# Keys and values of two row chunks by seven block products

## The chip, the cores and the metric

The kernel runs on one core of a Trainium2 chip. The metric is device time in microseconds (us), the median of several runs. A core has a matrix engine (TensorE, PE in the profile, with its weight loads as PEld), a vector engine (VectorE, DVE), a scalar engine (ScalarE, ACT), GpSimd (POOL) and a queue that only issues transfers here (SyncE, SP). Each works through its own list of instructions in order and waits on semaphores of the others. Tiles lie in SBUF; matmuls write to PSUM, in banks of 128x512 float32.

## The reference, cut to what matters

```python
# S = 2048 rows, D = 512, H = 32 heads of 16, F = 1792
q, k, v = x @ wqkv                        # per head
phi(t) = concat(softmax(t @ w_phi), softmax(-t @ w_phi))
kv = phi(k).T @ v ;  z = sum_s phi(k)     # per head, over all rows
a = (phi(q) @ kv / (phi(q) @ z + 1e-6)) @ wo
b = relu(x @ w1 + b1)**2 @ w2 + b2
g = sigmoid((x * gate_w).sum(-1))
out = g * a + (1 - g) * b
```

## The kernel before

Every large float32 product is made of three passes in the format float32r: an operand is split into a high part (a copy by ACT) and a low part (the operand minus the high part, by DVE), and `mm3` adds high times high, high times low and low times high in one PSUM bank. `split` is the line pair 61 and 64 of the profile.

The rows of x stand in four blocks (`NB`) of four chunks (`NC`) of 128 rows. The hidden width stands in 14 parts of 128; the work list runs over two sweeps of seven parts, four blocks each: 56 entries. For each entry `up` makes one 128x512 bank of the hidden layer (12 matmuls), two entries ahead (`LAG`), ACT and DVE make the squared relu and its split (`hidden`), and `down` adds 12 matmuls to four banks `d0` to `d3` that stay open for seven entries. This is the frame; everything of the attention is hung between by `at(slot, f)`, two slots for an entry.

In the first sweep that is keys and values. `do_fold` multiplies the key weights with the feature map (`fold`, plain float32 matmuls), `do_w` loads the value weights, and for each of the 16 chunks `do_k` makes 12 matmuls and `exps` (two reductions and two subtractions by DVE out of PSUM, an exponential by ACT, a sum and a reciprocal by DVE, then `scaled` on POOL, line 214), `do_v` makes 12 matmuls and one ACT copy into `vext` (line 411), and `do_kv` adds two chunks' 64 small matmuls to `kvps`. Keys and values take turns in one bank (`ps_a`; `ps_b` holds `kvps`), so the bank must be read out before the next of them starts. The second sweep does queries, numerators and the output projection in the same way.

What sets the order: the framework orders each engine's list from the program's order, with `high_priority(offset=AHEAD)` pulling the read-outs forward; what stands in the lists is fixed, and at run time an engine only waits. All loads and stores go through SP in order, into a ring of four staging tiles (`in`) and six `row` tiles.

Of the kernel before, what the change touches and what calls it, by code (L numbers as in the profile page):

```python
# [28 lines left out]
AHEAD = 150  # L29


@with_exitstack
def tile_gated_mix(ctx: ExitStack, tc: tile.TileContext, xT, xn, wqT, wkT, wphi, wv, wo, w1, b1, w2, b2, gw, out):
# [88 lines left out]
    part = dram.tile([NB * NC, P, D], F32, name="part")  # L122
    zrow = dram.tile([2 * D], F32, name="zrow")
# [15 lines left out]
    def fold(loaded, nm, k):  # L139
# [9 lines left out]
        return hi, lo  # L149

# [41 lines left out]
    def exps(ps, tag="e"):  # L192

        pv = ps.rearrange("p (h f) -> p h f", f=DH)
        mx = small.tile([P, H], F32, tag="mx", name="mx")
        mn = small.tile([P, H], F32, tag="mn", name="mn")
        e = work.tile([P, H, 2, DH], F32, tag=tag, name="e", bufs=2 if tag == "e" else 1)
        bc = lambda t: t.unsqueeze(2).to_broadcast([P, H, DH])
        with tc.high_priority(offset=AHEAD):
            nc.vector.tensor_reduce(mx, pv, AX.X, ALU.max)  # L200
            nc.vector.tensor_reduce(mn, pv, AX.X, ALU.min)
            nc.vector.tensor_tensor(e[:, :, 0, :], pv, bc(mx), ALU.subtract)
            nc.vector.tensor_tensor(e[:, :, 1, :], bc(mn), pv, ALU.subtract)  # L203
# [15 lines left out]
    def kv_chunk(n, kvps, phi, v):  # L219
        for i in range(NG):  # L220
            for j in range(4):
# [3 lines left out]
                                 start=(n == 0 and i == 0), stop=(n == NB * NC - 1),  # L225
# [86 lines left out]
    def up(fc, xs, wf):  # L312
        ps = ps_u.tile([P, SB], F32, tag="u", name="u")
        for k in range(NK):
            up_step(ps, k, xs, wf)
        return hidden(fc, ps)
# [8 lines left out]
    def do_fold(nm, k):  # L325
        with tc.issue_after(st["up"].ins):
            st["wa", nm, k] = fold(st["wT"], nm, k)
        if k == NK - 1:
            st["wa"] = [st["wa", nm, i] for i in range(NK)]
            if nm == "k":  # L330
                banks.pop()

# [69 lines left out]
    def do_k(b, c):  # L402

        n = b * NC + c
        e3, r = exps(project(c, st["x", b], st["wa"], "k"), "ez" if n % NV == NV - 1 else "e")
        st["phi", n] = scaled(e3, r, nc.gpsimd)

    def do_v(b, n, c):
        ps = project(c, st["x", b], st["wb"], "v")
        with tc.high_priority(offset=AHEAD):  # L410
            nc.scalar.activation(heads(vext[n % NV])[:, :, :DH], ps.rearrange("p (h f) -> p h f", f=DH), AF.Copy)

    def do_kv(n):
        if n == 0:
            st["kv"] = ps_b.tile([P, 2 * P], F32, tag="s", name="kvps")
        for m in (n, n + 1):
            kv_chunk(m, st["kv"], st["phi", m], vext[m % NV])
# [51 lines left out]
    def at(slot, f, *a):  # L469
        steps.setdefault(int(slot), []).append(lambda: f(*a))  # L470
# [7 lines left out]
    for k in range(NK):  # L478
        at(3 + k // 2, do_fold, "k", k)
    at(1, do_w, wv, "v")  # L480
    for b in range(NB):
# [5 lines left out]
        for c in range(NC):  # L487
# [128 lines left out]
```

## Time and profile before

| | |
|---|---|
| three runs | 530.46, 531.08, 531.87 us; median 531.08 |
| span of the profiled execution, first to last instruction | 528.2 us; no separate device time of that execution is listed, the median lies 2.9 us above its span |
| granted TensorE clock | 1.000 |
| busy: PE, PEld, DVE, ACT, POOL | 519.0, 417.6, 356.5, 234.1, 77.0 us |
| moved by the main queue | 44.20 MB, 26.8% of 16 engines' time |

The busy time of PE is a share of the span in which at least one matmul is under way; a matmul's row is longer than the distance to the next one, since they are pipelined. The distance between starts tells the rate. "Idle before" and the list of waits say who ended an engine's idle time. In a timeline a row gives start and duration in us; rows of one engine can overlap a little.

### The profile page before, as it was taken

The numbers are of one execution on the slowest core, as the hardware profiler recorded it, in microseconds if no ns is written. First come the engines' busy times: TensorE is split into PE (matmuls) and PEld (weight loads), VectorE is DVE, ScalarE is ACT, GpSimd is POOL, SyncE is SP. The second block draws the span as 40 slices with busy tenths as digits, with TensorE's granted clock in tenths as the row PEclk, the third lists the DMA queues.
The fourth block names the chain that finished last, engine by engine and source line by source line (L and its number), as shares of the span: only waits on it lengthen the run. The fifth ranks groups of instructions, "written<-read, shape, count | busy, mean of one in ns | idle before, by whom it ended". The sixth has DMA issues, their size and how long they took to land.

```text
span 528.2 us, 8945 instructions
## 1 busy us (share of the span) xinstructions
PE 519.0 (98%) x3475; PEld 417.6 (79%) x3475; DVE 356.5 (68%) x608; ACT 234.1 (44%) x404; POOL 77.0 (15%) x61
## 2 busy tenths in 40 slices
PE   8998999999999999999999999999999999999997
PEld 4876888888888888888878878787887878787785
DVE  4688546833656334566769897998878887779423
ACT  4874424623335234354644663463435353535230
POOL 2001111111111111011103121102011111112000
PEclk9999999999999999999999999999999999999999
DMA  7974004200032000434346114134102311022102
GB/s 255 297 234 131 1 1 161 81 2 1 24 138 79 2 0 22 159 85 137 81 146 215 34 40 124 66 107 130 45 17 89 113 49 30 24 77 94 47 1 79
DMA packets 30834, 45.16 MB, mean 86 GB/s; under 512 B 5704, under 2 KB 12360, under 8 KB 30792
## 3 DMA queue, kind: packets, MB, share of 16 engines
q1 hardware_dynamic: 30328, 44.20, 26.8%
q8 instruction: 27, 0.44, 0.4%
q10 hardware_dynamic: 432, 0.39, 0.2%
q14 instruction: 15, 0.12, 0.1%
q0 software_dynamic: 32, 0.01, 0.0%
HBM read 29.89 MB, written 8.39 MB: 72 GB/s over the span
## 4 chain that ended last, share of the span: by engine, by line
PE 63%; DVE 15%; DMA 7%; ACT 5%; SPq 5%; issue 2%; POOL 2%; DVEq 0%; POOLq 0%; ACTq 0%
PE u L69 6%; PE u L71 6%; PE u L70 6%; PE d L71 6%; PE d L70 6%; PE d L69 6%; SPq L259 4%; PE k L69 3%; PE v L69 2%; PE k L70 2%; PE k L71 2%; PE v L70 2%; PE v L71 2%; DMA in<-in_w 2%; PE att L69 2%
## 5 line engine op out<-in xcount | busy, mean ns | idle before, releaser
L305 ACT ACTIVATE r<-u,b1c 128x512 f32<-128x512 f32 x56 | 38.5, 687 | 152.1 <-PE u L71 143.5
L69 PE MATMUL d<-w2h,hh 128*128 128x512 f32 x224 | 87.5, 390 | 0.0
L69 PE MATMUL u<-xh,w1h 128*128 128x512 f32 x220 | 86.8, 395 | 0.4 <-ACT w1h L61 0.4
L70 PE MATMUL d<-w2l,hh 128*128 128x512 f32 x224 | 87.2, 389 | 0.0
L71 PE MATMUL d<-w2h,hl 128*128 128x512 f32 x224 | 87.2, 389 | 0.0
L71 PE MATMUL u<-xh,w1l 128*128 128x512 f32 x220 | 85.8, 390 | 0.1
L70 PE MATMUL u<-xl,w1h 128*128 128x512 f32 x220 | 85.7, 390 | 0.0
L64 DVE TENSOR_TENSOR hl<-r,hh 128x512 fp32r<-128x512 f32 x56 | 42.8, 764 | 55.9 <-ACT hh L61 55.9
L233 POOL TENSOR_TENSOR ez<-e,z 128x512 f32<-128x512 f32 x32 | 41.4, 1316 | 187.7 <-ACT e L205 187.7
L214 POOL TENSOR_TENSOR e<-e,r 128x1024 f32<-128x1024 f32 x16 | 32.4, 2025 | 202.1 <-DVE r L210 144.8
L208 DVE TENSOR_REDUCE sm<-e 128x64 f32<-128x1024 f32 x32 | 39.0, 1217 | 28.5 <-ACT e L205 28.3
L69 PEld LDWEIGHTS u<-xh,w1h 128*128 128x128 f32 x220 | 41.3, 188 | 12.2 <-ACT hh L61 1.6
L71 PEld LDWEIGHTS d<-w2h,hl 128*128 128x128 f32 x224 | 42.1, 188 | 8.7
L69 PEld LDWEIGHTS d<-w2h,hh 128*128 128x128 f32 x224 | 42.0, 188 | 8.7
L70 PEld LDWEIGHTS d<-w2l,hh 128*128 128x128 f32 x224 | 42.1, 188 | 8.6
L71 PEld LDWEIGHTS u<-xh,w1l 128*128 128x128 f32 x220 | 41.3, 188 | 9.1 <-DVE w1l L64 0.6
L70 PEld LDWEIGHTS u<-xl,w1h 128*128 128x128 f32 x220 | 41.3, 188 | 8.2
L205 ACT ACTIVATE e<-e 128x1024 f32<-128x1024 f32 x32 | 33.8, 1055 | 23.2 <-DVE e L203 22.4
L257 ACT ACTIVATE phiT<-tb 32x256 f32<-32x256 f32 x64 | 26.4, 413 | 34.6 <-DVE tb L251 33.9
L61 ACT ACTIVATE hh<-r 128x512 fp32r<-128x512 f32 x56 | 35.2, 628 | 1.3
L306 ACT ACTIVATE r<-r 128x512 f32<-128x512 f32 x56 | 35.1, 627 | 1.0
L566 DVE SCALAR_TENSOR_TENSOR row<-d,rest,row 128x512 f32<-128x512 f32 (+1 forms) x33 | 22.4, 731 | 8.5 <-PE d L71 8.5
(106 smaller groups left out, 875.4 us busy)
## 6 DMA issues: line engine op xcount, KB each, us to landing
in<-in_xT SPq DMA_DIRECT2D x32, 256.0 KB, 3.8
in<-in_w SPq DMA_DIRECT2D x24, 256.0 KB, 3.1
phiT<-tb SPq DMA_DIRECT2D x192, 32.0 KB, 1.8
row<-in_xn SPq DMA_DIRECT2D x16, 256.0 KB, 2.8
part<-row SPq DMA_DIRECT2D x16, 256.0 KB, 2.0
row<-part SPq DMA_DIRECT2D x16, 256.0 KB, 3.7
out<-row SPq DMA_DIRECT2D x15, 256.0 KB, 2.3
row<-in_wkT SPq DMA_DIRECT2D x4, 256.0 KB, 5.8
```

Of the source, the lines that this page charges most:

```text
L61: i = nc.scalar.activation(hi, src, AF.Copy)
L64: elo.tensor_tensor(lo, src, hi.bitcast(F32), ALU.subtract)
L69: nc.tensor.matmul(o, ah[:, sa], bh[:, sb], start=first, stop=False)
L70: nc.tensor.matmul(o, ah[:, sa], bl[:, sb], start=False, stop=False)
L71: return nc.tensor.matmul(o, al[:, sa], bh[:, sb], start=False, stop=last)
L205: nc.scalar.activation(ef, ef, AF.Exp)
L208: nc.vector.tensor_reduce(sm, e3, AX.X, ALU.add)
L214: eng.tensor_tensor(e3, e3, w.unsqueeze(2).to_broadcast([P, 2 * H, DH]), ALU.mult)
L233: nc.gpsimd.tensor_tensor(ez[:, hs, :], e3[:, hs, :], zbc[half], ALU.mult)
L257: nc.scalar.activation(dst, src, AF.Copy)
L305: nc.scalar.activation(r, ps, AF.Relu, bias=b1c[:, fc:fc + 1])
L306: nc.scalar.activation(r, r, AF.Square)
```

## The change

Two chunks c and c+2 of a block make a pair (eight in all). Their rows, cut in two halves of the inner width (256), are a 2x2 block matrix; the weights are laid side by side, half the columns of the folded key weights and half of the value weights in one 512-wide operand, and are a 2x2 block matrix too. Keys and values of a pair are then made by the Strassen-Winograd scheme: seven block products of six matmuls each, 42 instead of 48.

- `joint_weights` (slots 3 and 4) copies the folded keys out of PSUM beside the value columns (`raw`), splits seven operands for each half j, and makes four differences for each half on POOL (`sub`). Operands 1, 2, 5, 7 stay in SBUF (`HELD`); 6, 3 and 4 (`KEPT`) take turns in one place (`oh`, `ol`), are written to DRAM (`wkeep`), and are read back by `again` before each of their products: four transfers of 256 KB each, except for product 6 of pair 0.
- `sums` reads the pair's rows of x again from DRAM, makes four sums on POOL and splits them.
- `pair_steps` sets the products in the order 1, 2, 6, 5, 3, 7, 4, all in the bank of `ps_a`; 2 is added onto 1 and 4 onto 7 in the bank. `u2` and `u4` (`sums` tile) keep partial sums in SBUF. `place` writes the four results to the tiles `e` and `vext`, in halves of 16 heads (128x256).
- `exps` reads the keys from SBUF there, in place, and not from PSUM.
- Slots have halves now: a step may stand in the middle of `up` or after the second chunk of `down`.

```diff
-        at(3 + k // 2, do_fold, "k", k)
-    at(1, do_w, wv, "v")
+    at(3, do_joint, 0)
+    at(4, do_joint, 1)
...
+    def joint_weights(loaded):
...
+            r = raw[k] = work.tile([P, 2 * D], F32, tag="ez" if k == 1 else "e", name=f"raw{k}", bufs=1 if k == 1 else 2)
+            nc.sync.dma_start(two(r)[:, :, 256:], two(wv[k * P:(k + 1) * P, :]))
...
+            nc.scalar.activation(two(r)[:, :, :256], two(ps), AF.Copy)
...
+            split(src, hi, lo, nc.scalar, nc.vector)
+            st["W"][i, j] = hi, lo
+            if i in KEPT:
+                for hl, x in enumerate((hi, lo)):
+                    nc.sync.dma_start(wkeep[KEPT.index(i), j, hl], x.bitcast(F32))
...
+        def first(j):
+            whole(j)
+            whole(2 + j)
...
+            operand(1, j, a)
+            operand(2, j, c)
+            operand(3, j, d)
+            sub(a, b, a)
+            sub(b, d, b)
+            sub(d, d, a)
+            operand(5, j, a)
+            operand(7, j, b)
+            sub(c, c, d)
+            operand(4, j, c)
+            operand(6, j, d)
...
+    def sums(p):
...
+        nc.sync.dma_start(a, rows[:, :2])
+        nc.sync.dma_start(d, rows[:, 2:])
...
+        add(d1, a1, d1, ALU.add)
+        add(a1, a0, a1, ALU.subtract)
+        add(a0, d1, a0, ALU.subtract)
+        add(d0, d0, a0, ALU.subtract)
...
+        split(a, sh[:, 0], sl[:, 0], nc.scalar, nc.vector)
+        split(d, sh[:, 1], sl[:, 1], nc.scalar, nc.vector)
...
+    def again(i):
+        for j in range(2):
...
+                nc.sync.dma_start(x.bitcast(F32), wkeep[KEPT.index(i), j, hl])
...
+    def place(t, half, src, other=None):
...
+                if other is None:
+                    nc.scalar.activation(o, of(src), AF.Copy)
+                else:
+                    nc.vector.tensor_tensor(o, of(other), of(src), ALU.add)
...
+        at(s - 1, sums, p)
+        for off, f in zip((0, 1, 1.5, 2.5, 3.5, 4.5, 5), (p1, p2, p6, p5, p3, p7, p4)):
+            at(s + off, f)
+        at(s + 3.5, phi, n)
+        at(s + 5, phi, m)
+        at(s + 7.5, kv)
...
+    for p in range(NB * NC // 2):
+        pair_steps(p, 5.5 + 5.65 * p)
```

The lists of three engines show what the prediction speaks of. A name with a number is one buffer; "waits" names the engines or transfer semaphores a row waits for.

POOL, from the start of the kernel, before (`w1l0_130` is the low part of the first hidden weight, `e` the features of a chunk):

```order
L127 MEMSET vext2_110 128x32
L64 TENSOR_TENSOR w1l0_130<-row_128,w1h0_129 128x384 [waits DMAHW2_49,DVE_49]
L214 TENSOR_TENSOR e_470<-e_470,r_478 128x1024 [waits DVE_49,Activation_49]
L214 TENSOR_TENSOR e_557<-e_557,r_565 128x1024 [waits DVE_49,Activation_49]
L214 TENSOR_TENSOR e_655<-e_655,r_663 128x1024 [waits DVE_49,Activation_49]
```

The first feature scaling follows directly on the first hidden weight.

POOL at the same place, changed (`raw0` to `raw3` are the joint weights before their sums, `in_486` and `in_487` the rows of x of pair 0):

```order
L182 TENSOR_TENSOR raw0_328<-raw0_328 128x512 [waits DMAHW2_49,DVE_49]
L182 TENSOR_TENSOR raw0_328<-raw2_336,raw0_328 128x512 [waits DMAHW3_49,Pool_49]
L182 TENSOR_TENSOR raw2_336<-raw2_336,raw0_328 128x512 [waits DVE_49,Pool_49]
L182 TENSOR_TENSOR raw2_336<-raw2_336 128x512 [waits Pool_49]
L182 TENSOR_TENSOR raw1_400<-raw1_400 128x512 [waits DMAHW7_49,DVE_49]
L182 TENSOR_TENSOR raw1_400<-raw3_408,raw1_400 128x512 [waits DMAHW3_49,Activation_49,Pool_49]
L476 TENSOR_TENSOR in_487<-in_486,in_487 128x2x128 [waits DMAHW4_49,DMAHW6_49,DMAHW1_49,DVE_49]
L477 TENSOR_TENSOR in_486<-in_486 128x2x128 [waits DMAHW5_49,DMAHW0_49,Pool_49]
L478 TENSOR_TENSOR in_486<-in_487,in_486 128x2x128 [waits Pool_49]
L479 TENSOR_TENSOR in_487<-in_487,in_486 128x2x128 [waits Pool_49]
L182 TENSOR_TENSOR raw3_408<-raw3_408,raw1_400 128x512 [waits DVE_49]
L182 TENSOR_TENSOR raw3_408<-raw3_408 128x512 [waits Pool_49]
```

Twelve operations of POOL stand ahead of the first feature scaling that were not there.

PE, before, at the second chunk's keys (`k_542` is their bank, `wkh0` a part of the folded weights):

```order
L71 MATMUL d0_303<-w2h3_245,hl_342 128x512
L69 MATMUL d1_304<-w2h3_245,hh_341 128x512
L69 MATMUL k_542<-wkh0_356,xh0_0_136 128x512 [waits Activation_49]
L70 MATMUL k_542<-wkl0_357,xh0_0_136 128x512
L71 MATMUL k_542<-wkh0_356,xl0_0_137 128x512
L69 MATMUL k_542<-wkh1_365,xh0_1_153 128x512
```

Here PE waits for one thing, the read-out of the bank by ACT.

PE, changed, about the same number of matmuls from the start, at the second half of product 6 and the start of product 5 of pair 0 (`w61_448` and `w61_449` are high and low part of operand 6 for j = 1):

```order
L505 MATMUL p6_583<-w61_448,sh_494 128x512 [waits Activation_49]
L71 MATMUL u_613<-xh0_1_154,w1h6_542 128x512
L72 MATMUL u_613<-xl0_1_155,w1h6_542 128x512
L73 MATMUL u_613<-xh0_1_154,w1l6_543 128x512
L506 MATMUL p6_583<-w61_449,sh_494 128x512 [waits DVE_49]
L507 MATMUL p6_583<-w61_448,sl_495 128x512
L71 MATMUL u_613<-xh0_2_165,w1h6_542 128x512
L72 MATMUL u_613<-xl0_2_166,w1h6_542 128x512
L73 MATMUL u_613<-xh0_2_165,w1l6_543 128x512
L71 MATMUL u_613<-xh0_3_174,w1h6_542 128x512
L505 MATMUL p5_605<-w50_361,sh_494 128x512 [waits DVE_49]
```

PE now waits for the last weight that is made, high part by ACT and low part by DVE, and ahead of product 5 for DVE's read-out of the bank.

ACT in the middle of the first sweep, before (`v_1189` is a bank of values, `r` and `hh` the hidden layer, `e_1137` the features of a chunk):

```order
L205 ACTIVATE e_1137<-e_1137 128x1024 [waits DVE_49,Pool_49]
L305 ACTIVATE r_1182<-u_1169,b1c_98 128x512 [waits PE_49]
L306 ACTIVATE r_1182<-r_1182 128x512 [waits Activation_49]
L61 ACTIVATE hh_1185<-r_1182 128x512 [waits Activation_49]
L411 ACTIVATE vext2_110<-v_1189 128x32x16 [waits PE_49]
```

ACT in the middle of the first sweep, changed, at pair 3 (`p1_1397` is the bank of products 1 and 2, `e_1340` the features of pair 2's second chunk):

```order
L533 ACTIVATE sums_454<-p1_1397 128x512 [waits PE_49]
L260 ACTIVATE e_1340<-e_1340 128x1024 [waits DVE_49]
L360 ACTIVATE r_1418<-u_1405,b1c_98 128x512 [waits PE_49]
L361 ACTIVATE r_1418<-r_1418 128x512 [waits Activation_49]
L524 ACTIVATE e_1438<-p1_1397 128x16x16 [waits PE_49]
L524 ACTIVATE vext0_109<-p1_1397 128x16x16
```

Two read-outs of the bank enclose an exponential that waits for DVE.

176 lines of the change are left out of this document (138 added, 38 removed).

## The prediction

> **What bounds the kernel now.** First the page's busy times and the windows of the whole span, then PE's waits, then the rows of PE one by one.
>
> ```profile
> PE 519.0 (98%) x3475; PEld 417.6 (79%) x3475; DVE 356.5 (68%) x608; ACT 234.1 (44%) x404; POOL 77.0 (15%) x61
> ```
> ```profile
> 20.00:30.00 10.00, 9.75 (x58) 8.23 (x57) 8.24 (x18) 8.74 (x18) 0.00 (x0) 1.00 0.81 261
> 30.00:40.00 10.00, 10.00 (x45) 8.26 (x44) 8.66 (x23) 7.26 (x16) 0.00 (x0) 1.00 0.75 238
> 40.00:60.00 20.00, 18.58 (x81) 14.80 (x80) 16.01 (x41) 9.76 (x19) 3.87 (x2) 1.00 0.26 84
> 100.00:120.00 20.00, 20.00 (x90) 16.57 (x89) 9.09 (x17) 6.10 (x9) 1.94 (x1) 1.00 0.16 54
> ```
> ```profile
> PE k L69 <- ACT vext L411: 1.1, 1, 1.1
> PE v L69 <- DVE e L203: 0.3, 1, 0.3
> ```
> ```profile
> 29.46 0.48 PE L69 MATMUL u<-xh,w1h 128*128 128x512 f32 x1
> 48.77 0.39 PE L70 MATMUL d<-w2l,hh 128*128 128x512 f32 x1
> 58.74 0.39 PE L69 MATMUL k<-wkh,xh 128*128 128x512 f32 x1
> 61.23 0.39 PE L71 MATMUL k<-wkh,xl 128*128 128x512 f32 x1
> ```
>
> The columns of the windows are PE, PEld, DVE, ACT, POOL, clock, DMA share and GB/s. PE is full from 60 us on (100:120 stands for that stretch), and its waits in the first sweep are small. The keys' rows at 58.74 and 61.23 are eleven matmuls apart: 0.227 us each. So a matmul taken out is worth 0.227 us, and a wait put in costs its length: PE's order is fixed, and it has no slack to give a wait back. The other fact is 20 to 40 us: there ACT and DVE are over 70% busy and POOL does nothing. The change puts its new work exactly there.
>
> **The matmuls.** Eight pairs, six fewer each: 48 by 0.227 = 10.9 us less. The folds and the 64 small matmuls of a pair stay. If all else is covered the kernel ends at 520.2.
>
> **The start.** The first pair's products need weights made by ACT copies, splits and eight differences on POOL, and the pair's row sums (four more). The rows that price this:
>
> ```profile
> 25.14 0.58 ACT L61 ACTIVATE wkh<-foldk 128x512 fp32r<-128x512 f32 x1
> 28.41 0.68 DVE L64 TENSOR_TENSOR hl<-r,hh 128x512 fp32r<-128x512 f32 x1
> 29.01 0.69 DVE L64 TENSOR_TENSOR w2l<-in,w2h 128x512 fp32r<-128x512 f32 x1
> 44.61 2.23 DVE L64 TENSOR_TENSOR hl<-r,hh 128x512 fp32r<-128x512 f32 x1
> 253.00 0.63 DVE L64 TENSOR_TENSOR hl<-r,hh 128x512 fp32r<-128x512 f32 x1
> 253.55 2.42 DVE L64 TENSOR_TENSOR w2l<-in,w2h 128x512 fp32r<-128x512 f32 x1
> ```
> ```profile
> 44.36 1.93 POOL L214 TENSOR_TENSOR e<-e,r 128x1024 f32<-128x1024 f32 x1 [36.46 <-DVE ge L179]
> 253.25 2.17 POOL L214 TENSOR_TENSOR e<-e,r 128x1024 f32<-128x1024 f32 x1 [12.49 <-DVE r L210]
> ```
> ```profile
> L233 POOL TENSOR_TENSOR ez<-e,z 128x512 f32<-128x512 f32 x32 | 41.4, 1316 | 187.7 <-ACT e L205 187.7
> L64 POOL TENSOR_TENSOR w1l<-row,w1h 128x384 fp32r<-128x384 f32 x1 | 1.0, 1012 | 4.1 <-DVE w1h L63 4.1
> L208 DVE TENSOR_REDUCE sm<-e 128x64 f32<-128x1024 f32 x32 | 39.0, 1217 | 28.5 <-ACT e L205 28.3
> ```
>
> A low part on DVE takes 0.60 us when the next follows (28.41 to 29.01). But beside POOL it does not run: at 44.61 it began under a POOL operation that ended at 46.29 and finished at 46.84, 0.55 after it; at 253.25 POOL waited for the running DVE row, went ahead of the next one, and that one ended 0.55 after POOL. So the two take turns, one whole instruction each. This is told of operations with both inputs in SBUF, as all low parts here; reductions keep their 1217 ns.
>
> In the changed DVE list, from the first low part of a joint weight (`w10_345`) to the last (`w61_449`), 29 operations have two SBUF inputs: 25 low parts and four gate products. POOL's twelve must lie between them, for they need the first and the last needs them. ACT's first fold read-out stands at 25.14; in the new list three others follow before `w10` is copied, 0.52 apart, so DVE begins at about 27.4. POOL: eight of 1.30 (the 128x512 row) and four of 256 elements, about 0.7 (between 1.01 for 384 and half of 1.3): 13.2 us. DVE: 29 by 0.60 = 17.4 at most, with half a microsecond of tiny rows; where a turn changes, only some 0.40 are added (0.55 less the 0.15 by which POOL started early), so at least 12 by 0.40 and 17 by 0.60 = 15.0. The last weight is ready between 55.6 and 58.5 us. From there to the first matmul of product 5 are six matmuls or one read-out, 1.4 us: 57.1 to 60.0.
>
> That matmul is the 77th after the folds by the order, so 76 lie before it. The 77th of before is the row at 48.77, the first is that at 29.46. The second fold's start and length I leave as they are. The loss against before is therefore 8.3 to 11.2 us; I take 9.8, since nothing in the order prefers one end. Other steps are inside this: ACT has 36 rows from `w10` to `w61`, some 17 us by 0.52, less than the port's turns; the SP writes of operands 3 and 4 must land before the next one is split into the same place, 2.0 us each by the row below, while DVE works on other splits. If POOL were out of the way, these chains would be the bound (rival one).
>
> The Trainium skill, SBUF — State Buffer, section Who interferes with whom, says that a DVE instruction with two SBUF inputs and a GpSimd instruction that reads SBUF exclude each other, and the second to start fully blocks. It speaks against this change: by it the sum of the start is the 9.8 above, while POOL's idle column alone (nothing from 20 to 40 us) would give about 1.
>
> **The steady pairs.** One bank serves all seven products, so each product waits for the read-out of the one before.
>
> ```profile
> 61.66 0.69 DVE L200 TENSOR_REDUCE mx<-k 128x32 f32<-128x512 f32 x1 [3.13 <-PE k L71]
> ```
> ```profile
> 45.29 0.57 ACT L411 ACTIVATE vext<-v 128x512 f32<-128x512 f32 x1
> 45.92 0.50 PE L69 MATMUL k<-wkh,xh 128*128 128x512 f32 x1 [1.09 <-ACT vext L411]
> ```
> ```profile
> L205 ACT ACTIVATE e<-e 128x1024 f32<-128x1024 f32 x32 | 33.8, 1055 | 23.2 <-DVE e L203 22.4
> L411 ACT ACTIVATE vext<-v 128x512 f32<-128x512 f32 x16 | 9.5, 594 | 25.9 <-PE v L71 25.9
> L178 ACT ACTIVATE ge<-lg 128x1 f32<-128x1 f32 x16 | 3.0, 194 | 9.7 <-DVE row L176 9.7
> L566 DVE SCALAR_TENSOR_TENSOR row<-d,rest,row 128x256 f32<-128x256 f32 x2 | 0.9, 480 | 0.6 <-PE d L71 0.6
> ```
>
> A read-out starts 0.43 us after the last matmul's start (61.23 to 61.66), and PE goes on 0.06 after its end. Half a bank takes 0.39 us on ACT (between 194 and 594 ns) and 0.48 on DVE, so two halves need about 0.7 and 0.9. The order leaves at least six matmuls between, 1.59 us with the last one's own: enough for 1.10 us of read-out. An idle engine makes it.
>
> The place that fails is `place` of product 2 on ACT, with six matmuls behind it. In pairs 2, 3, 4, 6 and 7 the exponential of the pair before stands ahead of it. From the last matmul of product 4 (0): DVE reads it out to 1.3, POOL scales the other chunk from about 0.4 to 2.4, so the first of two low parts ends at 2.9, the next at 3.5, two reductions and two subtractions at 5.9, the exponential at 7.05, relu and square at 8.3, `place` at 9.05. Product 2 ends its matmuls at 6.8, 30 after; product 6 is due at 8.4. Late by 0.7; without POOL's turn it would be in time. Five pairs: 3.5 us. Ends: 0, and 6 if all eight are late by as much.
>
> DVE's other new work (two more low parts, two additions, six halves, some 5 us a pair) lies beside PE: a pair takes some 28 us and DVE is busy 9 of 20. ACT's and POOL's extra too. `exps` from SBUF has the same four operations.
>
> **The transfers.** 23 rereads of 1 MB, 3 MB of writes and 4 MB of x: 30 MB more in the first sweep.
>
> ```profile
> q1 hardware_dynamic: 30328, 44.20, 26.8%
> ```
> ```profile
> part<-row SPq DMA_DIRECT2D x16, 256.0 KB, 2.0
> row<-part SPq DMA_DIRECT2D x16, 256.0 KB, 3.7
> row<-in_wkT SPq DMA_DIRECT2D x4, 256.0 KB, 5.8
> ```
> ```profile
> 10.53 1.84 SPq L136 DMA_DIRECT2D row<-in_wkT  x4
> ```
>
> The tightest is operand 4 after product 3. SP issues four in 1.84 us, and a reread lands in 3.7: 5.5 us from the release after product 3. PE's fifth matmul of product 4 comes 28 matmuls after, 6.4 us. Slack 0.9, so 0. At 5.8 us to land, as four loads at once took at the start, each would be late by 1.2: 8 by 1.2 = 9.6 is the upper end. SP queues loads for the FFN behind a reread's wait for PE; those are needed slots later, so nothing is charged. The second sweep's code is the same: 0.
>
> **The sum.** The profiled span is 528.2 and the median of the runs 531.1, 2.9 above it; I add differences to the median: 531.1 - 10.9 + 9.8 + 3.5 = 533.5 us. Slower by 0.45%.
>
> One row bears on the stalls themselves:
>
> ```profile
> 1.19 4.88 PE L360 MATMUL warm<-zeros 128*128 128x512 bf16 x11 [1.19 <-DVE zeros L354]
> ```
>
> The first eleven matmuls stand 0.43 us apart, twice the later 0.227. If PE fell back to that for eleven after a long stall, it would cost 2.2 us; I take 0, because the last weight is what PE waits for anyway. The Trainium skill, TensorE: Matmul & The Clock Gate, Part 1, says that PE's clock halves after an idle window of about 3.4 us, which no later row of before shows (its longest PE wait is 1.2). By that page the sum would be some 535.
>
> **Rivals.** One, faster: POOL's operations fall where DVE waits for ACT or a landing, so they cost no turns. Speaking for it: DVE is 82 to 87% busy in that stretch, not 100. Against: 13 us of POOL do not fit into 13 to 18% of 30 us. Product 5 then starts between 46.7 (29.46 and 76 matmuls of 0.227, no wait) and some 50: x for the sums lands at about 39 (behind the writes of operand 4 on SP, 3.7 to land), six POOL operations, a copy, a write of 2.0, a copy and a low part follow, 9.3 in all, and 1.4 as above. That is -2.1 to 1 against 48.77; I take 1. Without turns the pairs are in time too: 531.1 - 10.9 + 1 + 0 to 1 = 521 to 522. It decides once the last weight is there before 50 us.
>
> Two, no change: the start is as forecast, but the pairs' exponentials end in time, because sums and scalings of POOL come at other moments than I assume: 531.1 - 10.9 + 9.8 = 530.0. For it: before's pairs wait nowhere between 60 and 240.
>
> Three, slower still: rereads land late, from about 4.6 us on. For it: 44.2 MB took 26.8% of 528 us, so 30 MB more take some 96 us of a sweep of about 250. With half the upper end, 533.5 + 4.8 = 538.
>
> **How the numbers follow.** Forecast 0.45, rival one 0.20, two 0.22, three 0.13. No change means within 0.3%, 1.6 us, about what these runs can tell. Faster: rival one and 0.04 of two, 0.24. Same: 0.17 of two and 0.07 of the forecast's low ends (start 8.3 and pairs 2 give 530.5), 0.24. Slower 0.52. The range leaves out most of rival one and the far end of three: 526 to 540. The forecast's own is 529 to 538.
>
> **What would show it.** POOL rows of the new differences between 28 and 55 us with DVE low parts of 1.2 to 2 us beside them; PE waits at `p1`, `p6` and for `w61` that add up to 10 to 13 us before 60; 42 matmuls a pair at 0.227; waits of `p6` on ACT of 0.5 to 1 in five pairs; none on transfers. It is wrong if PE's waits before 60 us are under 6, or if `p3`, `p4`, `p6` wait for `wkeep`.

## The result: 5.3% slower

| | before | changed |
|---|---|---|
| median of four runs | 531.25 us (530.46 to 531.87) | 559.38 us (556.63 to 561.08) |
| ratio to before, 95% interval | | 1.0526 (1.0495 to 1.0558) |
| profiled execution, time and span | | 560.0 and 558.1 us |

It was forecast at 533.5 us, 526 to 540: slower, the direction came out, the size missed by 25.9 us. The page of the changed kernel, then three of the windows shown for before and a fourth, 200:220 (PE, PEld, DVE, ACT, POOL, clock, DMA share, GB/s), with the row of before last:

```profile
PE 522.2 (94%) x3427; PEld 415.4 (74%) x3427; DVE 418.5 (75%) x694; ACT 248.8 (45%) x438; POOL 119.1 (21%) x101
...
PEclk9987998989998999999999999999999999999999
...
q1 hardware_dynamic: 54264, 75.66, 42.9%
```
```profile
30.00:40.00 10.00, 7.47 (x28) 5.38 (x27) 10.00 (x11) 5.94 (x11) 7.51 (x5) 0.89 0.56 193
40.00:60.00 20.00, 14.91 (x51) 11.19 (x50) 17.39 (x34) 11.20 (x25) 8.16 (x7) 0.80 0.74 237
100.00:120.00 20.00, 17.74 (x193) 13.93 (x192) 16.51 (x38) 9.54 (x20) 6.21 (x5) 0.91 0.67 211
200.00:220.00 20.00, 15.67 (x185) 12.60 (x184) 8.26 (x13) 4.85 (x7) 7.20 (x7) 0.91 0.29 99
```
```profile
200.00:220.00 20.00, 20.00 (x211) 16.46 (x211) 11.68 (x17) 5.42 (x8) 1.94 (x1) 1.00 0.31 97
```

PE has 48 matmuls fewer (3427 for 3475) and is busy 3 us longer, in part since it no longer runs at full clock all the way. The loss is not confined to 30 to 60 us: 100:120, where PE was full before, has 2.3 us of PE idle, and 200:220 has 4.3, with DVE busy 8.3 and ACT 4.9 of the 20 us beside it. The lists of waits of PE, SP and POOL say for what (us in total, number of waits, the longest):

```profile
PE kvps L278 <- POOL e L269: 12.7, 6, 4.3
PE p L505 <- ACT vext L524: 8.0, 5, 4.6
PE p L506 <- DVE w L66: 2.5, 1, 2.5
PE foldq L146 <- DVE vext L526: 2.2, 2, 1.5
```
```profile
SPq L490 <- PE p L507: 80.2, 26, 13.2
```
```profile
POOL in L476 <- DMA in<-in_xT: 39.3, 5, 16.7
```

The largest was in no term of the prediction: PE at `kv`, waiting for POOL to scale the features. SP stands 80 us before rereads that wait for PE, POOL 39 us before row sums whose x has not landed.

**An account by stage.** PE's matmuls start 0.227 us apart when nothing holds them. Summing what the distances exceed that (a matmul 0.38 to 0.45 from the next, the half-clock distance, is counted as cold) gives PE's lost time. The stages are 29 to 60 us, and from there to the transposes that end the first sweep. The lost time is that of the profiled execution, the time is the median.

| kernel | 29 to 60 us, of it cold | 60 us to sweep's end, of it cold | time, us |
|---|---|---|---|
| before | 2.0, 0 | 3.1, 0 | 531.3 |
| changed | 12.9, 3.6 | 29.8, 5.1 | 559.4 |
| kv late | 12.2, 3.6 | 29.4, 3.3 | 557.0 |
| no weight differences | 5.1, 0 | 28.6, 3.5 | 550.7 |
| differences on DVE | 7.5, 1.2 | 27.2, 4.3 | 551.5 |
| no rereads | 11.6, 2.6 | 22.3, 3.6 | 548.4 |
| small rereads | 11.8, 3.4 | 23.3, 2.2 | 552.6 |
| rereads that wait for nobody | 12.2, 2.6 | 24.1, 3.2 | 552.8 |
| no row sums | 10.5, 1.2 | 17.4, 1.8 | 545.3 |
| late start | 8.7, 2.4 | 20.3, 3.1 | 544.8 |
| late start, split kv | 7.9, 1.0 | 17.8, 1.8 | 544.5 |
| the same, sums on DVE | 3.4, 0 | 14.7, 0.2 | 535.9 |
| late start, no rereads, no sums | 3.1, 0 | 11.9, 0 | 530.7 |

Changed against before: 10.9 and 26.7 us more here, 1.8 more in the second sweep, 10.9 less for the matmuls: 28.5 of the 29.9 by which the span grew.

### The profile page after: what moved, and what is told of

Same layout as the page of the kernel before. It is cut to its first block, busy times and chain, and to the rows that moved or that the text cites. A ratio compares the mean times of both kernels' runs of the same rounds, so it can differ in the third digit from the quotient of the medians.

```text
span 558.1 us, 9288 instructions
## 1 busy us (share of the span) xinstructions
PE 522.2 (94%) x3427; PEld 415.4 (74%) x3427; DVE 418.5 (75%) x694; ACT 248.8 (45%) x438; POOL 119.1 (21%) x101
## 4 chain that ended last, share of the span: by engine, by line
PE 57%; DVE 17%; DMA 7%; ACT 5%; SPq 4%; POOL 4%; issue 4%; DVEq 0%; POOLq 0%
PE u L71 6%; PE d L73 6%; PE d L71 6%; PE d L72 6%; PE u L73 6%; PE u L72 5%; SPq L314 4%; DVE sm L263 3%; PE p L505 3%; DMA in<-in_xT 2%; PE att L73 2%; PE att L71 2%; PE p L506 2%; PE att L72 2%; PE p L507 2%
## 5 line engine op out<-in xcount | busy, mean ns | idle before, releaser
L73 PE MATMUL d<-w2h,hl 128*128 128x512 f32 x224 | 89.6, 400 | 0.0
L71 PE MATMUL d<-w2h,hh 128*128 128x512 f32 x224 | 89.4, 399 | 0.0
L72 PE MATMUL d<-w2l,hh 128*128 128x512 f32 x224 | 89.2, 398 | 0.0
L71 PE MATMUL u<-xh,w1h 128*128 128x512 f32 x220 | 88.2, 401 | 0.1
L269 POOL TENSOR_TENSOR e<-e,r 128x1024 f32<-128x1024 f32 x16 | 33.9, 2116 | 143.5 <-DVE r L265 98.2
L73 PEld LDWEIGHTS d<-w2h,hl 128*128 128x128 f32 x224 | 43.3, 193 | 9.3
L312 ACT ACTIVATE phiT<-tb 32x256 f32<-32x256 f32 x64 | 26.5, 414 | 37.8 <-DVE tb L306 37.2
```

Source lines behind the costliest of these rows:

```text
L71: nc.tensor.matmul(o, ah[:, sa], bh[:, sb], start=first, stop=False)
L72: nc.tensor.matmul(o, ah[:, sa], bl[:, sb], start=False, stop=False)
L73: return nc.tensor.matmul(o, al[:, sa], bh[:, sb], start=False, stop=last)
L269: eng.tensor_tensor(e3, e3, w.unsqueeze(2).to_broadcast([P, 2 * H, DH]), ALU.mult)
L312: nc.scalar.activation(dst, src, AF.Copy)
```

## The experiments

Times are medians; the kernel before ran beside every group at 530.8 to 531.3.

### The start: weights and turns

In the trace of the changed kernel POOL's differences and DVE's low parts stand side by side as forecast:

```profile
28.26 1.68 POOL L182 TENSOR_TENSOR raw<-raw 128x512 f32<-128x512 f32 x1 [20.36 <-DVE w L66]
30.01 3.32 POOL L182 TENSOR_TENSOR raw<-raw,raw 128x512 f32<-128x512 f32 x2
```
```profile
30.40 1.77 DVE L66 TENSOR_TENSOR xl<-in,xh 128x512 fp32r<-128x512 f32 x1
32.10 3.45 DVE L66 TENSOR_TENSOR w<-raw,w 128x512 fp32r<-128x512 f32 x2
```
```profile
58.79 0.50 PE L505 MATMUL p<-w,sh 128*128 128x512 f32 x1
```

A low part takes 1.7 us there for 0.6, and product 5 of pair 0 starts at 58.79, 10.0 after the row at 48.77 of before. PE's longest wait ahead of it, 4.6 us up to 50.0, is at product 6, for `place` of product 2 on ACT; in ACT's list that stands behind copies of the row sums, which wait for POOL:

```profile
46.09 0.63 ACT L63 ACTIVATE sh<-in 128x512 fp32r<-128x512 f32 x1 [2.73 <-POOL in L478]
...
49.31 0.36 ACT L524 ACTIVATE e<-p 128x256 f32<-128x256 f32 x1
```

**No differences.** `sub` does nothing.

```diff
         def sub(o, a, b):
-            nc.gpsimd.tensor_tensor(o, a, b, ALU.subtract)
+            pass
```


> The eight differences of raw joint weights on POOL are left out; the operands are copies of undiffered weights, in the same order and with all splits and writes. Theory of the turns: without these 13 us of POOL beside them DVE's low parts run on, product 5 of pair 0 starts near 50 us and not at 58.8, the half-speed stretches before 60 us go: 7 to 12 us less than 559.4, 547 to 552. Rival: ACT's copies and the writes of operands 3 and 4 are a chain almost as long, and product 5 starts no earlier than 56: 0 to 3 us less.

Measured 550.7 us (8.7 less), product 5 at 50.50. So POOL's eight rows cost about what was forecast for them, their own length and the turns together; copies and writes alone would have let the start through.

**Differences on DVE.**

```diff
-            nc.gpsimd.tensor_tensor(o, a, b, ALU.subtract)
+            nc.vector.tensor_tensor(o, a, b, ALU.subtract)
```


> The eight differences of joint weights are made by DVE and not by POOL; the rest is the changed kernel. Theory of the turns: DVE has 37 two-input operations of 0.6 to 0.7 us in the stretch and only POOL's four sums beside them, so the last weight is ready some 4 to 7 us earlier, product 5 of pair 0 starts at 52 to 55 and not at 58.8, and the time falls by as much, 551 to 556. Rival: the length of the list is what counts, whichever engine makes them, and product 5 starts at 57 to 60: 557 to 561.

Measured 551.5 us (7.9 less), product 5 at 56.0, later than expected by 1, but with eleven more matmuls (2.5 us) ahead of it in PE's list than in the changed kernel. The differences are the same, and the gain in time is nearly the whole one. DVE's rows in the same place:

```profile
31.48 0.68 DVE L182 TENSOR_TENSOR raw<-raw,raw 128x512 f32<-128x512 f32 x1
32.08 0.68 DVE L66 TENSOR_TENSOR w<-raw,w 128x512 fp32r<-128x512 f32 x1
32.68 0.68 DVE L182 TENSOR_TENSOR raw<-raw 128x512 f32<-128x512 f32 x1
```

They run 0.60 apart: between 27.25 and 36.4 DVE does fifteen such rows, where the changed kernel did seven with POOL beside them. The Trainium skill, SBUF — State Buffer, section Who interferes with whom, has a DVE instruction with two SBUF inputs contend with a GpSimd instruction that reads SBUF, under an exclusive lock; the two traces agree.

**Late start.** Weights are made when they were; the pairs begin three slots later and follow closer.

```diff
-        at(s + 7.5, kv)
+        at(s + (9 if p < 7 else 7), kv)
...
-        pair_steps(p, 5.5 + 5.65 * p)
+        pair_steps(p, 8.5 + 5.3 * p)
```
(with the differences on DVE)

> The differences on DVE (alone 551.5), the first pair three slots later, 5.3 slots between pairs for 5.65, kv one and a half slots later than in the changed kernel (half a slot earlier for the last pair); weights are made when they were. Theory of the start: FFN matmuls, of which there are enough, cover the making of the weights; PE's excess of 7.5 us between 29 and 60 us falls to about 2, and kv gains its slack: 540 to 547. Rival: the closer pairs pay it back at the read-outs of the one bank: 549 to 556.

Measured 544.8 us, 6.7 less than with the differences on DVE alone. PE's lost time before 60 us did not fall (8.7 for 7.5: the wait moved to 50 to 54 us, where product 6 stood 3.8 us behind ACT's `place`); the gain is in the pairs, 20.3 for 27.2. The range held, the place named in it did not.

### The wait at kv

The second chunk of pair 3, from its last subtraction to `kv`, in the changed kernel, engine by engine:

```profile
165.28 0.69 DVE L258 TENSOR_TENSOR e<-e,mx 128x512 f32<-128x512 f32 x1
169.30 0.69 DVE L227 SCALAR_TENSOR_TENSOR row<-row,gwb 128x512 f32<-128x512 f32 x1 [3.33 <-DMA row<-in_xn]
...
169.92 1.21 DVE L263 TENSOR_REDUCE sm<-e 128x64 f32<-128x1024 f32 x1
...
171.65 0.54 DVE L265 RECIPROCAL r<-sm 128x64 f32<-128x64 f32 x1
```
```profile
167.48 1.04 ACT L260 ACTIVATE e<-e 128x1024 f32<-128x1024 f32 x1
```
```profile
172.36 2.23 POOL L269 TENSOR_TENSOR e<-e,r 128x1024 f32<-128x1024 f32 x1 [11.22 <-DVE ge L230]
```
```profile
174.65 1.06 PE L278 MATMUL kvps<-e,vext 128*17 128x32 f32 x64 [2.74 <-POOL e L269]
```

The exponential is done at 168.5; DVE's sum stands behind a gate product (line 227) that waits for its row of x and ends at 170.0, 1.5 us after the exponential, so POOL starts at 172.4, after the reciprocal (the releaser named is the tiny row behind it), and PE gets the features at 174.6. Before, the same chain had time to spare; the scaling of the last chunk, and the `kv` that uses it:

```profile
139.65 1.94 POOL L214 TENSOR_TENSOR e<-e,r 128x1024 f32<-128x1024 f32 x1 [11.86 <-DVE r L210]
```
```profile
152.94 1.29 PE L223 MATMUL kvps<-e,vext 128*17 128x32 f32 x128
```

From 141.6 to the second chunk's half of `kv` are 11.9 us; over the eight pairs this slack is 9.5 to 11.9. In the changed kernel it is 0.1 to 0.2 in seven pairs and 1.4 in one: PE waits at nearly every `kv`. The slots say why: `do_kv` stood five slots behind the second chunk's keys, `kv` stands two and a half behind product 4, which finishes them.

**kv late.**

```diff
-        at(s + 7.5, kv)
+        at(s + (9.5 if p < 7 else 7.5), kv)
```


> The kv products of a pair (kvps) are set two slots, 24 FFN matmuls or some 5.5 us, later for the first seven pairs; nothing else is moved. Theory: PE's 12.7 us of waits for POOL's scaling (line 269), and four of the clock's half-speed stretches that follow them (3.4 us each, 1.7 us lost each), go: 14 to 20 us less than the changed kernel's 559.4, so 539 to 545. Rival A: only the waits go and the clock halves elsewhere (at p1 and p6): 545 to 548. Rival B: PE meets the next read-out earlier instead and waits there: 555 to 560.

Measured 557.0 us: 2.4 less, about the least that these runs can tell; rival B. The slack is back (6.1 to 11.1 us in those seven pairs), and PE waits elsewhere for as long:

```profile
PE p L505 <- DVE vext L526: 6.8, 7, 3.2
PE p L505 <- ACT vext L524: 5.9, 2, 3.0
```
```profile
97.22 0.69 DVE L227 SCALAR_TENSOR_TENSOR row<-row,gwb 128x512 f32<-128x512 f32 x1 [2.34 <-DMA row<-in_xn]
...
97.84 0.41 DVE L526 TENSOR_TENSOR e<-sums,p 128x256 f32<-128x256 f32 x1
```
```profile
98.64 0.50 PE L505 MATMUL p<-w40h,xh 128*128 128x512 f32 x1 [3.24 <-DVE vext L526]
```

Here the read-out of product 7 stands behind a gate product that waits for a load, and product 4 behind the read-out. So the kv wait was where lateness showed, not the whole of where it came from. My theory of it as a separate loss falls.

**kv early, before.** Does such a wait come by itself when `kv` is early?

```diff
-                at(s + 5, do_kv, n - 1)
+                at(s + (3 if n < 15 else 5), do_kv, n - 1)
```


> The kernel before, with its kv products two slots (some 5.5 us) earlier for the first seven pairs, so that PE waits there for POOL's scaling as the changed kernel does. Theory: a wait of 2 to 4 us at each of seven pairs, and a half-speed stretch of the clock of some 3.4 us behind each wait of over 2 us, 1.7 us lost each: 531.3 plus 14 to 28 plus up to 12, so 545 to 570, with the mean granted clock below 1. Rival: the waits come without a fall of the clock: 545 to 560 with the clock at 1.000. If the features are ready in time all the same there is no wait and no change.

Measured 530.7 us, ratio 0.999 (0.998 to 0.9999): no wait. The slack falls to 1.3 to 3.8 us and stays positive; before's features come early enough even so.

**PE busy at kv.**

```diff
             for t in (n, m):
+                if t == m and p in (0, 1, 3, 4):
+                    wh = st["W"][1, 0][0]
+                    for q in range(16):
+                        nc.tensor.matmul(st["kvbank"][:, 2 * P:], wh[:, :P], wh[:, :2 * P], ...)
```


> The changed kernel with 16 extra matmuls of 256 columns (some 1.8 us) between the two halves of kv in pairs 0, 1, 3 and 4, into unused columns of the kv bank. They fill a part of the waits for POOL that stand there (2.2 to 4.5 us). Theory: the half-speed stretches follow from PE standing idle for over 2 us; three or four of them go, 1.7 us each, and the extra matmuls lie in time that was waited: 4 to 7 us less than 559.4, 552 to 555.5. Rival: the clock falls for another reason, or the waits move on by as much: 558 to 563.

Measured 557.2 us (553.5 to 558.2), ratio 1.0476 (1.0429 to 1.0524), which overlaps the changed kernel's interval: no gain that these runs can tell. The granted clock rose in all four runs (0.990 to 0.993, for 0.977 to 0.984), and in the profile the half-speed stretches after 60 us are gone (cold time 5.1 to 0) and the kv waits fall from 12.7 to 6.6; the 64 extra matmuls last 2.0 us in each of four pairs, 8.1 in all, and take most of it back.

### The transfers

**No rereads.**

```diff
-        if i in KEPT and (p, i) != (0, 6):
-            again(i)
...
-            wh, wl = st["W"][i, j]
+            wh, wl = st["W"][6 if i in KEPT else i, j]
```


> The rereads of wkeep from DRAM are left out, 23 MB; products 6, 3 and 4 all use the operand that already lies there. Writes stay. Theory: no wait on them was seen, so 0, within 2 us of 559.4. Rival: they delay the x reads of the pair sums and the FFN loads on the one queue, and so POOL and the kv products: 5 to 10 us less.

Measured 548.4 us: 11.0 less. The theory (0) was wrong. PE never waited 0.5 us for a reread in the changed kernel, yet they cost 11 us, through what stands behind them: without them POOL's waits for the landing of x rows fall from 39.3 to 4.1 us.

**Small rereads, and rereads that wait for nobody.**

```diff
-                nc.sync.dma_start(x.bitcast(F32), wkeep[KEPT.index(i), j, hl])
+                nc.sync.dma_start(x[:, :8].bitcast(F32), wkeep[KEPT.index(i), j, hl, :, :8])
```


> Each reread stays on SP at its place and waits for PE as before, but fetches 8 of 512 columns, 16 KB for 1 MB, into the operand that lies there. The kernel without rereads took 548.4. Theory of the queue (a reread that waits for PE holds back the rows of x, the gate rows and the partial stores behind it): the waits are all there, so hardly a gain, 555 to 561. Rival, the theory of the traffic (23 MB more make the landings slow): as without rereads, 546 to 551.

```diff
-                nc.sync.dma_start(x.bitcast(F32), wkeep[KEPT.index(i), j, hl])
+                nc.sync.dma_start(spare[p, KEPT.index(i), j, hl], wkeep[KEPT.index(i), j, hl])
```


> The converse: 23 MB of rereads are issued on SP at the same places, but from wkeep to a DRAM place of their own that nobody reads, so none waits for PE; products 6, 3 and 4 use the operand that lies there. Theory of the queue: as without rereads, 546 to 552. Rival, the theory of the traffic: 555 to 562.

Measured 552.6 and 552.8, between theory and rival both times. Taking the traffic away and keeping SP's waits gains 6.8 us, taking the waits away and keeping the traffic 6.6. So each matters; whether the two overlap (13.4 for 11.0) is within the spread of these runs.

**Gate rows and stores on ACT's queue.**

```diff
-        nc.sync.dma_start(st["xn", n], xn[n])
+        nc.scalar.dma_start(st["xn", n], xn[n])
...
-                    (nc.scalar if j else nc.sync).dma_start(dst[:, s], o[:, s])
+                    (nc.scalar if j or sw == 0 else nc.sync).dma_start(dst[:, s], o[:, s])
```
(with kv late)

> The kv products late as in the run with late kv alone (557.0), and the gate's row loads and the stores of the partial sums issued by ACT's queue, out of the rereads' way; rereads stay on SP. Theory of the queue: DVE's waits for gate rows (2 to 3 us) and ACT's for a row tile whose store is late (4.2 us) go, and PE's waits for the read-outs behind them: 6 to 12 us less, 545 to 551. Rival: ACT's issuing costs as much as it saves, 554 to 559.

Measured 566.4 us, 9.3 more than kv late alone, against both. The issue waits for a free `row` tile, and now ACT waits with it, between the two halves of a relu:

```profile
96.41 0.34 ACTq L222 DMA_DIRECT2D row<-in_xn  x1
96.80 0.63 ACT L361 ACTIVATE r<-r 128x512 f32<-128x512 f32 x1 [1.50 <-DMA part<-row]
```

**Rereads, before.** The other way round: the kernel before is given 22 rereads of 1 MB.

```diff
         n = b * NC + c
+        again(0, st["wa"], n)
...
+        if n % 2 == 0:
+            again(1, st["wb"], n)
         ps = project(c, st["x", b], st["wb"], "v")
```


> The kernel before, with 22 rereads of 1 MB added on SP: half of the folded key weights (for 15 chunks) and of the value weights (for 7) are written to DRAM once and read back into their place between uses, so that each waits for PE there and holds back what is behind it. Theory, that rereads cost by themselves: 4 to 11 us slower than 531.1, 535 to 542. Rival: the kernel before has the slack to take them (its kv products could come 5.5 us earlier without a wait), so the cost in the changed kernel comes from its long chain of steps: 530 to 533.

Measured 531.4 us, ratio 1.0009 (0.9997 to 1.0021): nearly the same bytes, and waits of SP for PE of 92.5 us in all for 80.2, cost at most some 1.1 us there. The scaling and the `kv` of the same pair as above:

```profile
142.69 1.94 POOL L215 TENSOR_TENSOR e<-e,r 128x1024 f32<-128x1024 f32 x1 [11.86 <-DVE r L211]
```
```profile
155.98 1.21 PE L224 MATMUL kvps<-e,vext 128*17 128x32 f32 x120
```

The slack is still 10.0 to 11.9 us. So a reread has no price of its own in that kernel; that it costs where the steps behind it have no time left fits both kernels.

### The row sums

**No row sums.**

```diff
-        at(s - 1, sums, p)
...
-                h, l = st["S", p][i][j]
+                h, l = (t[:, cs] for t in x[j + 2 * (i < 6)])
```


> The row sums of a pair are left out: no second read of x (4 MB), no additions on POOL, no split of them; products 6, 7, 3 and 5 use rows of x that are there. The rest is the changed kernel with its rereads. Theory: POOL's scaling stands behind additions that wait up to 16.7 us for x rows, and DVE's chain behind their low parts; PE's 12.7 us at kv fall to under 5 and the time by 6 to 12 us, 547 to 553. Rival: they lie beside PE and their removal changes at most the start: 555 to 559.

Measured 545.3 us: 14.1 less, more than expected; the kv waits fall from 12.7 to 5.1 and the pairs' lost time from 29.8 to 17.4.

**Sums without loads.** The same additions, copies and low parts, but from x tiles in SBUF.

```diff
-        nc.sync.dma_start(a, rows[:, :2])
-        nc.sync.dma_start(d, rows[:, 2:])
...
-        add(d1, a1, d1, ALU.add)
+        add(d1, c0, c1, ALU.add)
```


> The row sums of the changed kernel with all their additions, copies and low parts, but made from x tiles that lie in SBUF: the second read of x (4 MB) and the wait for it are gone. With the sums left out wholly the time was 545.3. Theory of the late loads: POOL's scaling and DVE's chain stand behind additions that wait for x rows to land, so most of the 14 us comes: 545 to 551. Rival: it is the work of POOL, ACT and DVE itself that fills the chain: 555 to 559.

Measured 557.1 us, the rival's range. The run does not separate the two cleanly: without the wait for x, POOL makes the sums of pair 1 and the first of pair 2 from 49.1 to 55.5, beside DVE's rows, which take up to 1.2 us there for 0.7; PE waits 5.5 us at product 6 for the last weight, product 5 starts at 62.7, 3.9 later, and only the pairs gain (29.8 to 24.4). Of the 12.4 that the pairs gain without sums, the late x and its bytes would then be some 5.4, and the larger part the work on POOL, DVE and ACT: an estimate, since the start moved too.

**Later features, split kv** (on the late start).

```diff
-        at(s + 3.5, phi, n)
-        at(s + 5, phi, m)
-        at(s + (9 if p < 7 else 7), kv)
+        at(s + (4.5 if p < 7 else 3.5), phi, n)
+        at(s + (6.5 if p < 7 else 5), phi, m)
+        at(s + (9 if p < 7 else 6), kv, n)
+        at(s + (11 if p < 7 else 7), kv, m)
```


> On the late start (544.8): the features of a pair's first chunk one slot and of the second one and a half slots later, so behind the pair's own last read-outs and not between them, and kv in two halves, the first chunk's at slot 9, the second's at 11 of the pair; the last pair's features stay, its first kv half comes one slot earlier. Theory: read-outs of the one bank wait behind reductions and the exponential; without those in between PE's 12.5 us of waits at the products fall by 4 to 8: 537 to 541. Rival: the features now meet the read-outs of the next pair instead: 543 to 548.

Measured 544.5 us, for 544.8: the rival, nothing gained.

**Sums on DVE** (on the split kv).

```diff
-        add = nc.gpsimd.tensor_tensor
+        add = nc.vector.tensor_tensor
```


> On the split kv (544.5): the four row sums of a pair are made by DVE, some 0.4 us each, and not by POOL, which then has the scaling alone. Theory of the turns: DVE's two-input rows no longer wait for four POOL rows a pair, 541 to 543. Rival: DVE, in order, now stands itself before x rows that have not landed, and the read-outs behind it: 546 to 552.

Measured 535.9 us: 8.5 less by moving 32 small additions from POOL to DVE, well past the theory's range. Both stages gain (7.9 to 3.4 and 17.8 to 14.7), the clock no longer falls before the end, and no wait of PE in the pairs is over 1.5:

```profile
PE p L505 <- DVE vext L526: 2.1, 4, 1.5
...
PE p L505 <- ACT vext L524: 1.9, 2, 1.1
```

Some 4.5 us of it come at the start. ACT's copy of the row sums, ahead of `place` of product 2, waits less for them, first with the sums on POOL, then with the sums on DVE, and PE's wait at product 6 falls from 3.6 to 1.1:

```profile
52.30 0.63 ACT L63 ACTIVATE sh<-in 128x512 fp32r<-128x512 f32 x1 [3.47 <-POOL in L478]
```
```profile
49.86 0.63 ACT L63 ACTIVATE sh<-in 128x512 fp32r<-128x512 f32 x1 [1.08 <-DVE in L478]
```

The turns do not show as the reason: summed from 29 us to the sweep's end, DVE's two-input rows run 14.0 us over the shortest of their kind in the split kv and 14.4 here. What gave the pairs their 3.1 us is not shown.

It is the fastest of the kernels that do the whole computation by seven products, and still slower than before: ratio 1.0093 (1.0056 to 1.0131).

### What is left, and what 48 matmuls are worth

**Three edits together** (kv late, no rereads, differences on DVE).

```diff
-        at(s + 7.5, kv)
+        at(s + (9.5 if p < 7 else 7.5), kv)
...
-            nc.gpsimd.tensor_tensor(o, a, b, ALU.subtract)
+            nc.vector.tensor_tensor(o, a, b, ALU.subtract)
...
-            again(i)
```


> Three edits in one: kv products two slots late (alone 557.0), no rereads, with products 6, 3 and 4 on the operand that lies there (alone 548.4), and the eight weight differences on DVE (alone 551.5). If the three causes are separate, the gains add: 559.4 - 2.4 - 11.0 - 7.9 = 538. Theory of the chain (late loads and the early kv hold each other up: kv's wait only moved because DVE and ACT stood behind late loads): the kv waits go for good, 530 to 537. Rival: seven products through one bank wait for ACT's and DVE's read-outs anyway, 541 to 547.

Measured 543.3 us; the sum of the gains was 538. The rival: kv has its slack, and PE waits for read-outs of the one bank:

```profile
PE p L503 <- DVE vext L524: 7.9, 8, 1.9
```

**Late start, no rereads, no sums** (the products use rows and operands that are there).

```diff
-        at(s - 1, sums, p)
...
-            again(i)
...
-        pair_steps(p, 5.5 + 5.65 * p)
+        pair_steps(p, 8.5 + 5.3 * p)
```


> On the late start (544.8): neither rereads nor row sums; products 6, 3, 4 use the operand that lies there, products 6, 7, 3, 5 rows of x that are there. What is left is the seven products, their read-outs and the weights made at the start. Theory: what ate the gain is what the scheme needs around the products; without it the pairs run at 0.227 us per matmul but for some 5 us: 531.3 - 10.9 + 2 to 5 at the start + 5 = 527 to 531. Rival: seven read-outs of one bank per pair cost by themselves: 535 to 541.

Measured 530.7 us, ratio 1.0001 (0.9983 to 1.0018): the upper end of the theory. With rereads and row sums taken away, the seven products with their read-outs, the placing and the start still eat the 10.9 us that they save: 11.9 for 3.1 in the pairs, 3.1 for 2.0 at the start, 2.1 in the second sweep. The largest group of PE's waits is again DVE's read-outs, 5.3 us in five; the one of 1.7 ends at 92.4, where the read-out stood behind the sum of a chunk's features.

**Before, 48 matmuls fewer.**

```diff
-        for k in range(NK):
-            mm3(ps, xs[k], ws[k], sc, ALL, k == 0, k == NK - 1)
+        last = NK // 2 if nm == "v" and c % 2 else NK
+        for k in range(last):
+            mm3(ps, xs[k], ws[k], sc, ALL, k == 0, k == last - 1)
```


> The kernel before with 48 matmuls fewer and nothing else: the values of every second chunk are summed over half of the inner width only, 6 matmuls for 12. Theory: a matmul on the path is worth 0.227 us, so 531.3 - 10.9 = 520.4, 519.5 to 521.5. Rival: read-outs of the one bank come closer together and take some of it back, 523 to 527.

Measured 522.1 us (520.2 to 524.0), ratio 0.9831 (0.9803 to 0.9858): 8.8 less, a little short of the theory. The pairs lose no more than before (3.2 for 3.1); the start loses 1.8 more, of it 1.4 in a half-speed stretch.

## Why the prediction was wrong, step by step

**The matmuls: nearly held.** 10.9 forecast, 8.8 when nothing else is changed (interval 7.5 to 10.5, from 0.0142 to 0.0197 of 531); PE's distances in the pairs are 0.227 as before.

**The start: the number held, PE's path did not.** 9.8 forecast, 10.0 at product 5 of pair 0; the last weight was ready at 56.5, inside the forecast 55.6 to 58.5, and taking POOL's differences away gave 8.3 of the 10.0 back. The POOL row was dearer (1.6 to 1.8 us for 1.30). But PE never waited for that weight: it lost 4.6 us at product 6 of pair 0, for `place` of product 2, 2.5 for a low part of product 1's weight and 3.6 at half clock, and came to the last weight after it was ready. That the sum is the forecast one is partly luck.

**The steady pairs: the step that failed.** Its 3.5 us, bounds 0 to 6, stand against 26.7, of it 5.1 at half clock. What it priced came in part: `place` of product 2 late behind ACT's exponential of the features, 1.8 us in pairs 2 to 4 (1.2 in pair 3, 0.2 to 0.3 in the others, not 0.7 in the five named). Another 1.6 in pair 1 look the same in the list of waits, but ACT stood there before the gate's small exponential, which waited for DVE's gate product; the features' exponential comes behind `place`:

```profile
78.31 0.20 ACT L229 ACTIVATE ge<-lg 128x1 f32<-128x1 f32 x1 [4.92 <-DVE row L227]
78.42 0.37 ACT L524 ACTIVATE e<-p 128x256 f32<-128x256 f32 x1
```

What it left out was the chain through the pair. It took `kv` as given ("the 64 small matmuls of a pair stay") and never set the features' ready time against kv's new slot: 12.7 us of waits. "An idle engine makes it" was the same omission at the read-outs: DVE was counted 9 of 20 us busy, but its list is in order, and a read-out can stand behind a reduction, a low part or a gate product that itself waits. The run with kv late shows that the two hang together: mend the first and the second appears. "ACT's and POOL's extra too" put the row sums at nothing as well; without them the time was 14.1 us less, and with them on DVE, on the split kv, 8.5 less.

**The transfers: 0 was wrong, for another reason than rival three's.** No product waited for `wkeep`, as forecast; still the rereads cost 11.0 us and the rows of x for the sums some more (5.4 by the estimate above). The failing sentence is that the loads which SP queues behind a reread "are needed slots later, so nothing is charged". They are needed later by PE, but sooner by DVE and POOL, which work ahead of it: SP's 80 us of waiting stand ahead of the loads on which POOL waited 39 us and DVE at the gate products.

**The clock: 0 was wrong.** Cold matmuls cost 8.7 us more than before, 3.6 at the start and 5.1 in the pairs. The prediction had the row (0.43 us apart) and the price of one stretch, 2.2, and took 0 because PE waits for the last weight anyway; that covers the start at best, and nothing of the pairs.

**The signs to look for** named POOL's rows, `p1`, `p6`, `w61`, `wkeep`. POOL's and DVE's rows came out as written, and nothing waited for `wkeep`. PE's waits before 60 us added up to 7.6, not 10 to 13, with none for `w61`, and `p6` waited for ACT in four pairs after the start and not five, once for another reason; but 7.6 is over the 6 below which the forecast was to count as wrong. The list had no line for `kv`, so nothing on it could fail there.

**What stays open.** How much of the last 8.8 us in the pairs is the single bank and how much DVE's list: a second bank was not tried. How the row sums cost the pairs: by late x, by the work on POOL, DVE and ACT, or by the turns. And what the clock alone costs: the run that kept PE busy could not tell.

## What to carry to other kernels

When a change moves a consumer in a fixed order, find for each of its inputs when the producer's last row ended before and how many us were to spare; here some 10 us of slack at `kv` were spent in the diff by two numbers, and giving them back alone gained 2.4 us, because the read-outs behind had none either. The 23 MB of rereads cost 11.0 us there; 22 MB in the kernel that had the slack cost at most some 1.1. Fewer matmuls on the full engine are a gain only if the work that makes them possible goes to engines whose in-order lists, not whose busy shares, have room.

## What the runs showed of the hardware

The granted clock of PE fell to half for stretches of 3.41 us, each behind an idle time of about 2.0 to 4.6 us, as the windows around the wait of pair 3 at `kv` show (clock third from the end):

```profile
171.00:174.40 3.40, 0.91 (x5) 0.41 (x3) 2.90 (x12) 0.20 (x1) 2.04 (x1) 0.99 0.83 269
174.40:177.80 3.40, 3.15 (x69) 2.70 (x70) 0.00 (x0) 0.00 (x0) 0.20 (x1) 0.50 0.57 196
177.80:181.20 3.40, 3.40 (x16) 2.80 (x16) 0.69 (x1) 0.00 (x0) 0.00 (x0) 1.00 0.00 0
```

Before the last instruction there are six spells of it in the changed kernel (from 37.8, 48.1, 85.6, 116.3, 174.4 and 208.5 us, the second of double length), whole multiples of 3.41 apart. A wait of 2.0 us between the two halves of `kv`, which are 64 matmuls of 32 columns each, was enough (it ended at 115.0); one of 2.6 in the run with PE busy was not:

```profile
169.22 0.73 PE L278 MATMUL kvps<-e,vext 128*17 128x32 f32 x64 [2.62 <-POOL e L269]
```

What tells them apart is how they lie on that grid. Cut on it, the windows that hold the wait of 2.0 and one at 201.7 in the changed kernel, then the two that share the wait of 2.6 in the run with PE busy:

```profile
112.93:116.34 3.41, 1.43 (x81) 1.16 (x68) 3.41 (x6) 0.00 (x0) 2.05 (x1) 1.00 0.91 279
116.34:119.75 3.41, 3.41 (x10) 2.63 (x9) 1.16 (x7) 2.34 (x5) 1.86 (x3) 0.50 0.65 187
201.68:205.09 3.41, 1.56 (x68) 1.01 (x67) 2.49 (x4) 2.72 (x4) 3.18 (x5) 1.00 0.82 285
205.09:208.50 3.41, 0.93 (x65) 0.88 (x66) 0.64 (x1) 0.00 (x0) 2.42 (x2) 1.00 0.04 14
```
```profile
165.02:168.43 3.41, 1.57 (x12) 1.14 (x10) 3.06 (x11) 0.20 (x1) 1.50 (x1) 1.00 0.33 91
168.43:171.85 3.42, 2.63 (x72) 2.23 (x73) 0.69 (x1) 0.00 (x0) 0.73 (x1) 1.00 0.57 180
```

In these two traces, from 20 us to the end, every window of the grid in which PE was busy 1.48 us or less was followed by half clock, and none with 1.56 or more was. The edge is not exact: in the split kv a window with 1.96 us was followed too.

The Trainium skill, TensorE: Matmul & The Clock Gate, Part 1, puts it down to a window of 3413 ns that runs free and looks at how busy PE was; the grid agrees. Its limit for idle gaps, some 3.4 us, is not what the traces show: 2.0 us sufficed.
